# Transposing gathered rows on TensorE with a copy on ScalarE in place of a DMA transpose

## The chip, the cores and the metric

The kernel runs on one core of a Trainium2 chip. The metric is the device time of one execution in microseconds (us). The engines are TensorE (PE), VectorE (DVE), ScalarE (ACT), GpSimd (POOL) and SyncE (SP); SP issues DMAs here, and POOL issues the indirect ones. Each engine works through its own queue in order. An "L" with a number is a line of the kernel.

## The reference

Three layers in a row: attention in chunks of 64 rows, a mixture of 8 experts where each token goes to the expert with the highest gate value, and a feed-forward block (FFN). The change lies in the middle one. x has 2304 tokens of 512 values, an expert's first weight is 512x1024, its second 1024x512.

```python
expert_idx = np.argmax(logits, axis=1)
# the first `capacity` (576) tokens of each expert, in order: disp[e, pos] = x[i]
h = np.maximum(np.einsum('ecd,edf->ecf', disp, w1), 0.0)
y = np.einsum('ecf,efd->ecd', h, w2)
for i in range(N):
    if keep[i]:
        out[i] = gate_w[i] * y[expert_idx[i], pos[i]]
# then FFN: h = x @ w_in; g = h * sigmoid(h); g @ w_out
```

All values are float32 at the inputs. The kernel multiplies in float16 and gets the accuracy from splitting each number into a high and a low half (hi, lo): three products hi·hi, lo·hi and hi·lo per block.

## The kernel before

The attention stage writes the rows of x, split in two f16 halves of 512 values (1024 f16 values and one factor per row), to DRAM (x_d), and a router makes tables of which tokens belong to which expert. The stage of the experts runs from some 143 to 437 us, the FFN from there to the end.

**Tiles.** An expert's tokens are worked on in tiles of 128 rows; a tile is (e, j), expert e and tile j. At most 5 tiles of each expert (NJ) are written out in code; tile (e, 0) always runs, tile (e, j) for j from 1 on stands under a branch on the expert's count (`more`, L930), and a loop (`rest`) takes what lies past them. With this input the experts have 4, 1, 4, 3, 2, 1, 3 and 2 tiles, 20 in all.

A tile goes like this. `gather` (L819, POOL, indirect DMA) fetches 128 rows of x_d into one of four buffers xg. `t_dma` (L830, SP) starts a DMA transpose of the 128x1024 f16 values into mxT, of which there are three, so that the 512 values lie on partitions. `t_f1` (L826, DVE) works out a factor. Layer 1 on PE: 96 matmuls 128x128x128 (L845) in two halves into PSUM tiles mh. After each half ScalarE writes hh (L850), and DVE hl (L851), the high and low half of the rectified result. Layer 2 on PE: 24 matmuls 128x512 (L866) into myp, for f from 0 to 7 two with hh and one with hl; f 0 to 3 use the first half's hh and hl, f 4 to 7 the second's. Then ScalarE and DVE split the result into yr (L874 to L879), and POOL scatters it to y_d (L882).

**What runs beside it.** While an expert is worked on, the weights of the experts behind it are made ready. SP loads a weight as four pieces of 512 KB into buffers st (L134 the first weight, L136 the second). ScalarE squares each piece (L157, result "junk") with a row sum; PE adds these over partitions (L124, `total`); DVE makes a scale of it (L102 to L104); POOL writes the high half in f16 (L172); DVE the low half (L175), after which the buffer st may be loaded again. In the same way DVE rebuilds pieces of the FFN's weights (L794 to L802, buffers fs, loaded by L779; L808 is a square of them on ScalarE). Which piece stands where is laid down by hand: `moe_tile` calls `bg(0)` to `bg(4)` and `nxt(-1)` to `nxt(1)` at fixed places (start of tile; after the first half of layer 1; behind layer 1; at f = 6 of layer 2), and lists of functions (`slots`, `arms`) hang on those. For tile (e, 0), nxt is `nxt0`, for the others the `nxt` of `more`.

**Where the transposes stand.** The DMA transpose of tile (e, j+1) is issued at the start of tile (e, j); that of (e+1, 0) behind layer 1 of (e, 0), ahead of loads of the first weight of expert e+2 in SP's queue. The first, the second and expert 7's second stand apart. Each is also issued for the tile behind an expert's last, which is not run: 28 in this run. Ahead of the first tile 28 matmuls with constants (L927) warm PE up.

**PSUM.** fh_s holds two banks for the FFN, fh0 and fh1; while the experts run, fh0 takes the sums of L124 and fh1 is free.

In the attention stage the kernel already transposes 128x1024 f16 rows on PE, eight blocks (L439), with a copy out of PSUM on DVE or ScalarE (L444).

Of the kernel before, what the change touches and what calls it, by code (L numbers as in the profile page):

```python
# [9 lines left out]
F16 = mybir.dt.float16  # L10
# [12 lines left out]
def attention_moe_ffn_kernel(  # L23
# [15 lines left out]
    nc = tc.nc  # L39
    B, H, S, D = q.shape  # L40
    NT, DM = out.shape
    E = w_gate.shape[1]
    DF1 = w1.shape[2]
    DFF = w_in.shape[1]
    P = 128
# [7 lines left out]
    NJ = 5  # L53
# [716 lines left out]
    ps_s = [mps.tile([P, 4, P], F32, name=f"mh{i}") for i in range(4)]  # L770
    yp_s = [mps.tile([P, DM], F32, name=f"myp{i}") for i in range(2)]

    def f_load(k):
        if k >= 2 * KFF:
            return
        m, c = divmod(k, KFF)
        t = fs_s[k % 3]
        if m == 0:
            nc.sync.dma_start(  # L779
                out=t.rearrange("p (k f) w -> p k (f w)", k=KD),  # L780
                in_=w_in.bitcast(I32).rearrange("(k p) f -> p k f", p=P)[:, :, c * 2 * P:(c + 1) * 2 * P],
            )
        else:
            nc.sync.dma_start(out=t.rearrange("p f w -> p (f w)"), in_=w_out.bitcast(I32)[c * P:(c + 1) * P, :])
# [29 lines left out]
    def slot(e, j):  # L814
        return 2 if j % 2 else e % 2
# [9 lines left out]
        f1 = f1_s[slot(e, j)]  # L825
        nc.vector.tensor_scalar(f1, xg[:, DM:DM + 1], w_fac[e, 0], w_fac[e, 1], ALU.mult, ALU.mult)  # L826

    def t_dma(e, j):
        xg = xg_s[2 * (e % 2) + j % 2]
        nc.sync.dma_start_transpose(out=xT_s[slot(e, j)], in_=xg.bitcast(F16)[:, 0:2 * DM])  # L830

    def moe_tile(e, j, tok_i, c_i, keep, nxt, bg):
        xt, f1 = xT_s[slot(e, j)], f1_s[slot(e, j)]
# [24 lines left out]
        yp = yp_s[1 if j else 0]  # L858
        n = 0
        for f in range(KF1):  # L860
            if f == 3 * KF1 // 4:
                bg(4)
                nxt(1)
            hh, hl = hs[f // 4]
            for lh, part in ((hh, 0), (hh, 1), (hl, 0)):
                nc.tensor.matmul(  # L866
                    out=yp, lhsT=lh[:, f % 4, :], rhs=b[f // 2][:, part, (f % 2) * DM:(f % 2 + 1) * DM],
                    start=(n == 0), stop=(n == 3 * KF1 - 1),
                )
                n += 1  # L870
# [20 lines left out]
        gather(e, j, tabs[:, 0, e, j:j + 1])  # L891

    def t_next(e, j):
        t_dma(e, j)
        t_f1(e, j)

    def rest(e):
# [16 lines left out]
    t_next(0, 0)  # L914
    g_next(0, 1)
    g_next(1, 0)
    t_dma(0, 1)
    w_load(1, 1)
    p10[1]()
    g_next(0, 2)  # L920
# [8 lines left out]
    def more(e, j, arms):  # L929
        with tc.If(n_e[e] > P * j) as cmp:  # L930
            def nxt(k):
                if k < 0 and j + 1 < NJ:
                    t_dma(e, j + 1)
                if k == 0 and j + 1 < NJ:
                    t_f1(e, j + 1)
                if k == 0 and j + 2 < NJ:
                    g_next(e, j + 2)

            moe_tile(
                e, j, *cols(e, j), nxt,  # L940
                lambda k: [f() for f in arms[j][k]],
            )
            if j + 1 < NJ:
                more(e, j + 1, arms)
            else:
                with tc.If(n_e[e] > P * NJ):
                    rest(e)
        left = arms[0] if j == 1 else [f for i in range(j, NJ) for k in range(5) for f in arms[i][k]]
        if left:
            with cmp.Else():  # L950
                for f in left:
                    f()
# [28 lines left out]
    for e in range(E):  # L981
# [23 lines left out]

        def nxt0(k):
            if k < 0:
                if 0 < e < E - 1:
                    t_dma(e, 1)
            elif k == 0:  # L1010
                t_f1(e, 1)
                if last:
                    g_next(e, 2)
                else:
                    t_dma(e + 1, 0)
            elif not last:
                t_f1(e + 1, 0)
            else:
                with tc.If(n_e[e] <= SPLIT0):
                    y0_fac()  # L1020
# [16 lines left out]
            arms[0] = []  # L1037
        more(e, 1, arms)
        if e + 2 == E:
            t_dma(E - 1, 1)  # L1040
            with tc.If(n_e[E - 1] <= SPLIT0):
                y0_load()
    with tc.If(n_e[E - 1] > SPLIT0):
# [211 lines left out]
```

## Time and profile before

| | |
|---|---|
| median of 3 runs | 850.56 us (850.43 to 857.25) |
| profiled execution | 850.38 us, its span in the trace 848.6 us |
| mean granted clock of TensorE | 0.929 |
| busy, us: PE, PE weight loads, DVE, ACT, POOL | 722.5, 440.5, 448.1, 333.2, 359.4 |
| DMA | 103.20 MB, mean 122 GB/s |

The trace holds one execution. A busy time sums an engine's instructions; a wait is the idle time ahead of an instruction, put down to what came last. "x8" behind a row counts instructions that were joined in it. The granted clock is a share of full speed: TensorE has two levels here, 1.2 and 2.4 GHz, shown as 0.50 and 1.00, and means in between.

### The profile page before, as it was taken

The numbers are of one execution on the slowest core, as the hardware profiler recorded it, in microseconds if no ns is written. First come the engines' busy times: TensorE is split into PE (matmuls) and PEld (weight loads), VectorE is DVE, ScalarE is ACT, GpSimd is POOL, SyncE is SP. The second block draws the span as 40 slices with busy tenths as digits, with TensorE's granted clock in tenths as the row PEclk, the third lists the DMA queues.
The fourth block names the chain that finished last, engine by engine and source line by source line (L and its number), as shares of the span: only waits on it lengthen the run. The fifth ranks groups of instructions, "written<-read, shape, count | busy, mean of one in ns | idle before, by whom it ended". The sixth has DMA issues, their size and how long they took to land.

```text
span 848.6 us, 14692 instructions
## 1 busy us (share of the span) xinstructions
PE 722.5 (85%) x5526; PEld 440.5 (52%) x5526; DVE 448.1 (53%) x920; ACT 333.2 (39%) x615; POOL 359.4 (42%) x355
## 2 busy tenths in 40 slices
PE   4798764998489989569798776999999999999995
PEld 3677654765456756447553333444444444565442
DVE  4365886654794758678339999633322223222000
ACT  5586737443443536442134455322232223223010
POOL 3475632524571737665167535544223223212111
PEclk9797955899699999979899999999999999999999
DMA  7988983992986798895635235020001000001000
GB/s 170 230 231 206 191 239 59 306 273 56 303 246 162 177 235 239 241 237 123 135 72 102 73 125 124 1 51 1 1 37 38 1 1 37 14 1 39 13 37 38
DMA packets 133325, 103.20 MB, mean 122 GB/s; under 512 B 85472, under 2 KB 112096, under 8 KB 133216
## 3 DMA queue, kind: packets, MB, share of 16 engines
q1 hardware_dynamic: 126784, 83.41, 40.2%
q0 software_dynamic: 5760, 18.39, 7.3%
q8 instruction: 60, 0.98, 0.5%
q14 instruction: 49, 0.40, 0.2%
q10 hardware_dynamic: 672, 0.02, 0.0%
HBM read 73.45 MB, written 14.71 MB: 104 GB/s over the span
## 4 chain that ended last, share of the span: by engine, by line
PE 30%; DVE 8%; issue 7%; DMA 4%; POOL 2%; ACT 1%; POOLq 0%; ACTq 0%; DVEq 0%
PE ops L1143 14%; PE fh L1115 14%; DMA out_dram<-ob,yrow 3%; DVE g L1126 2%; DVE th L1121 2%; DVE wot L797 1%; DVE wot L802 1%; PE mh L845 1%; DVE wot L794 1%; DVE win L734 1%; DMA y_d<-yr,tabs 1%; PE myp L866 0%; POOL win L751 0%; POOL win L749 0%; POOL win L750 0%
## 5 line engine op out<-in xcount | busy, mean ns | idle before, releaser
L1143 PE MATMUL ops<-wot,gh 128*128 128x512 f16 x576 | 171.3, 379 | 0.0
L1115 PE MATMUL fh<-yT,win 128*128 128x512 f16 (+1 forms) x768 | 156.9, 355 | 7.0 <-DVE g L1126 7.0
L1130 POOL TENSOR_TENSOR gl<-g,gh 128x512 f16<-128x512 f32 (+1 forms) x80 | 91.9, 1151 | 163.8 <-ACT gh L1128 163.8
L1115 PEld LDWEIGHTS <-win 128*128 128x128 f16 x960 | 94.2, 98 | 118.1 <-issue 26.1
L845 PE MATMUL mh<-mxT,wsp 128*128 128x128 f16 x1920 | 125.6, 233 | 17.7 <-PEq L930 9.4
L845 PEld LDWEIGHTS <-wsp 128*128 128x128 f16 x1920 | 123.5, 106 | 24.1 <-issue 19.9
L1143 PE MATMUL ops<-wot,gl 128*128 128x512 f16 x288 | 109.2, 379 | 0.0
L1121 DVE TENSOR_TENSOR th<-fh,rb 128x512 f32<-128x512 f32 (+1 forms) x64 | 39.8, 622 | 130.7 <-PE fh L1115 130.7
L1122 ACT ACTIVATE th<-th,fi 128x512 f32<-128x512 f32 (+1 forms) x80 | 54.3, 679 | 133.8 <-DVE th L1121 132.9
L175 DVE SCALAR_TENSOR_TENSOR wsp<-st,s,wsp 128x1024 f16<-128x1024 f32 x64 | 99.6, 1591 | 6.0 <-POOL wsp L172 6.0
L866 PE MATMUL myp<-wsp,hh 128*128 128x512 f16 x320 | 96.5, 384 | 0.0
L1143 PEld LDWEIGHTS <-gh 128*128 128x128 f16 x576 | 56.4, 98 | 64.1
L172 POOL TENSOR_SCALAR wsp<-st,s 128x1024 f16<-128x1024 f32 x56 | 75.2, 1359 | 20.0 <-DVE inv L104 11.4
L1128 ACT CAST gh<-g 128x512 f16<-128x512 f32 (+1 forms) x80 | 45.9, 574 | 73.2 <-DVE g L1126 54.3
L157 ACT ACTIVATE junk<-st 128x1024 bf16<-128x1024 f32 x64 | 67.4, 1053 | 16.4 <-DMA st<-in_moe_w_dram 15.3
L1126 DVE TENSOR_TENSOR g<-fh,th 128x512 f32<-128x512 f32 (+1 forms) x80 | 50.7, 634 | 38.8 <-ACT th L1122 32.4
L866 PE MATMUL myp<-wsp,hl 128*128 128x512 f16 x160 | 61.6, 385 | 8.2 <-DVE hl L851 8.0
L819 POOL DMA_INDIRECT xg<-x_d,tabs x34 | 45.4, 1336 | 35.2 <-issue 9.5
L882 POOL DMA_INDIRECT y_d<-yr,tabs x20 | 23.5, 1175 | 79.3 <-DVE yr L879 36.8
L851 DVE SCALAR_TENSOR_TENSOR hl<-mh,hh 128x512 f16<-128x512 f32 x40 | 27.5, 687 | 48.3 <-ACT hh L850 48.3
L1115 PE MATMUL fh<-st,win 128*128 128x512 f16 x192 | 43.5, 379 | 10.6 <-DVE g L1126 9.3
L866 PEld LDWEIGHTS <-hh 128*128 128x128 f16 x320 | 30.7, 101 | 29.8 <-ACT hh L850 0.8
(194 smaller groups left out, 849.8 us busy)
## 6 DMA issues: line engine op xcount, KB each, us to landing
st<-in_moe_w_dram SPq DMA_DIRECT2D x64, 512.0 KB, 6.4
fs<-in_moe_w_in_dram SPq DMA_DIRECT2D x16, 512.0 KB, 7.0
fs<-in_moe_w_out_dram SPq DMA_DIRECT2D x16, 512.0 KB, 3.4
vbd<-in_v_dram SPq DMA_DIRECT2D x72, 64.0 KB, 3.4
x_d<-xr SPq DMA_DIRECT2D x9, 512.0 KB, 6.1
ku<-in_k_dram SPq DMA_DIRECT2D x6, 512.0 KB, 5.7
qu<-in_q_dram SPq DMA_DIRECT2D x6, 512.0 KB, 8.3
ku<-in_k_dram SPq DMA_DIRECT2D x2, 384.0 KB, 4.2
```

What stands on the lines that cost most here:

```text
L157: nc.scalar.activation(out=junk, in_=st[c], func=ACTF.Square, accum_out=n2[:, c:c + 1])
L172: hi_eng.tensor_scalar(sp[c][:, 0, :], st[c], s, 1.0, ALU.mult, ALU.mult)
L175: lo_eng.scalar_tensor_tensor(out=sp[c][:, 1, :], in0=st[c], scalar=s, in1=sp[c][:, 0, :], op0=ALU.mult, op1=ALU.subtract)
L845: nc.tensor.matmul(out=ps[:, f4, :], lhsT=a[c][:, part, f0:f0 + P], rhs=xt[:, rc, :], start=(n == 0), stop=(n == 3 * KD - 1),)
L866: nc.tensor.matmul(out=yp, lhsT=lh[:, f % 4, :], rhs=b[f // 2][:, part, (f % 2) * DM:(f % 2 + 1) * DM], start=(n == 0), stop=(n == 3 * KF1 ...
L1115: nc.tensor.matmul(out=hp[:, 0:n], lhsT=wv[:, part, c, :], rhs=yT_t[b](rc, n), start=(i == 0), stop=(i == 3 * KD - 1),)
L1121: nc.vector.tensor_tensor(out=th[:, 0:n], in0=hp[:, 0:n], in1=rb_t[b][:, 0:n], op=ALU.mult)
L1122: nc.scalar.activation(out=th[:, 0:n], in_=th[:, 0:n], func=ACTF.Sigmoid, scale=fi[:, 0:1])
L1126: nc.vector.tensor_tensor(out=g[:, 0:n], in0=hp[:, 0:n], in1=th[:, 0:n], op=ALU.mult)
L1128: nc.scalar.copy(out=gh[:, 0:n], in_=g[:, 0:n])
L1130: nc.gpsimd.tensor_tensor(out=gl[:, 0:n], in0=g[:, 0:n], in1=gh[:, 0:n], op=ALU.subtract)
L1143: nc.tensor.matmul(out=o_t[b][t], lhsT=lh[:, t * P:(t + 1) * P], rhs=wv[:, part, :], start=(f == 0 and i == 0), stop=(f == KFF - 1 and i = ...
```

## The change

`t_dma` is taken out wherever it stood. `x_tr(e, j)` takes its place: eight transposes on PE with the identity as the other operand, into a PSUM tile of one bank (xtp, which is fh1 seen as f16), and one copy of 128x1024 f16 by ScalarE to mxT. The transpose of (e, j+1) now stands behind layer 1 of (e, j), and that of (e+1, 0) at a new place, `nxt(2)`, ahead of f = 4 of layer 2 in (e, 0). That of (0, 0) stands ahead of the warm-up matmuls. Numbers of lines behind the edit move by 2 to 6: layer 1 is L849, layer 2 L872, the transposes are L833 and the copy L834.

```diff
@@ -770,6 +770,8 @@
     ps_s = [mps.tile([P, 4, P], F32, name=f"mh{i}") for i in range(4)]
     yp_s = [mps.tile([P, DM], F32, name=f"myp{i}") for i in range(2)]
 
+    xtp = fh_s[1].bitcast(F16).rearrange("p (c t) -> p c t", c=2 * KD)
+
     def f_load(k):
         if k >= 2 * KFF:
             return
@@ -825,9 +827,11 @@
         f1 = f1_s[slot(e, j)]
         nc.vector.tensor_scalar(f1, xg[:, DM:DM + 1], w_fac[e, 0], w_fac[e, 1], ALU.mult, ALU.mult)
 
-    def t_dma(e, j):
-        xg = xg_s[2 * (e % 2) + j % 2]
-        nc.sync.dma_start_transpose(out=xT_s[slot(e, j)], in_=xg.bitcast(F16)[:, 0:2 * DM])
+    def x_tr(e, j):
+        xh = xg_s[2 * (e % 2) + j % 2].bitcast(F16)
+        for c in range(2 * KD):
+            nc.tensor.transpose(out=xtp[:, c, :], in_=xh[:, c * P:(c + 1) * P], identity=ident16)
+        nc.scalar.copy(out=xT_s[slot(e, j)], in_=xtp)
 
     def moe_tile(e, j, tok_i, c_i, keep, nxt, bg):
         xt, f1 = xT_s[slot(e, j)], f1_s[slot(e, j)]
@@ -858,6 +862,8 @@
         yp = yp_s[1 if j else 0]
         n = 0
         for f in range(KF1):
+            if f == KF1 // 2:
+                nxt(2)
             if f == 3 * KF1 // 4:
                 bg(4)
                 nxt(1)
@@ -891,7 +897,7 @@
         gather(e, j, tabs[:, 0, e, j:j + 1])
 
     def t_next(e, j):
-        t_dma(e, j)
+        x_tr(e, j)
         t_f1(e, j)
 
     def rest(e):
@@ -914,7 +920,6 @@
     t_next(0, 0)
     g_next(0, 1)
     g_next(1, 0)
-    t_dma(0, 1)
     w_load(1, 1)
     p10[1]()
     g_next(0, 2)
@@ -929,9 +934,8 @@
     def more(e, j, arms):
         with tc.If(n_e[e] > P * j) as cmp:
             def nxt(k):
-                if k < 0 and j + 1 < NJ:
-                    t_dma(e, j + 1)
                 if k == 0 and j + 1 < NJ:
+                    x_tr(e, j + 1)
                     t_f1(e, j + 1)
                 if k == 0 and j + 2 < NJ:
                     g_next(e, j + 2)
@@ -1005,14 +1009,15 @@
 
         def nxt0(k):
             if k < 0:
-                if 0 < e < E - 1:
-                    t_dma(e, 1)
-            elif k == 0:
+                return
+            if k == 0:
+                x_tr(e, 1)
                 t_f1(e, 1)
                 if last:
                     g_next(e, 2)
-                else:
-                    t_dma(e + 1, 0)
+            elif k == 2:
+                if not last:
+                    x_tr(e + 1, 0)
             elif not last:
                 t_f1(e + 1, 0)
             else:
@@ -1037,7 +1042,6 @@
             arms[0] = []
         more(e, 1, arms)
         if e + 2 == E:
-            t_dma(E - 1, 1)
             with tc.If(n_e[E - 1] <= SPLIT0):
                 y0_load()
     with tc.If(n_e[E - 1] > SPLIT0):
```

SP's queue, with tile (0, 0), before; st_66 to st_69 are the pieces of expert 2's first weight, xg_2145 is the gather of tile (1, 0), xg_2143 that of (0, 2):

```order
L134 DMA st_66<-in_moe_w_dram 128x1024
L830 DMA_TRANSPOSE mxT_2148<-xg_2145 128x8x128
L134 DMA st_67<-in_moe_w_dram 128x1024
L134 DMA st_68<-in_moe_w_dram 128x1024
L134 DMA st_69<-in_moe_w_dram 128x1024
L930 COMPARE_AND_BRANCH
L830 DMA_TRANSPOSE mxT_2147<-xg_2143 128x8x128
L136 DMA st_70<-in_moe_w_dram 128x2x512
```

The same place after:

```order
L134 DMA st_66<-in_moe_w_dram 128x1024
L134 DMA st_67<-in_moe_w_dram 128x1024
L134 DMA st_68<-in_moe_w_dram 128x1024
L134 DMA st_69<-in_moe_w_dram 128x1024
L935 COMPARE_AND_BRANCH
L136 DMA st_70<-in_moe_w_dram 128x2x512
```

Both transposes are gone from between the loads, and nothing in SP's queue waits for a gather any more.

ScalarE's queue in the same tile, before (hh_2153 and hh_2154 are the two halves of the layer-1 output, st_70 to st_73 the pieces whose squares it takes):

```order
L850 ACTIVATE hh_2153<-mh_2168 128x512
L157 ACTIVATE junk,n_1757<-st_70 128x1024
L157 ACTIVATE junk,n_1757<-st_71 128x1024
L850 ACTIVATE hh_2154<-mh_2169 128x512
L157 ACTIVATE junk,n_1757<-st_72 128x1024
L157 ACTIVATE junk,n_1757<-st_73 128x1024
```

After:

```order
L854 ACTIVATE hh_2153<-mh_2168 128x512
L157 ACTIVATE junk,n_1757<-st_70 128x1024
L157 ACTIVATE junk,n_1757<-st_71 128x1024
L854 ACTIVATE hh_2154<-mh_2169 128x512
L834 COPY mxT_2149<-fh_2136 128x1024
L157 ACTIVATE junk,n_1757<-st_72 128x1024
L157 ACTIVATE junk,n_1757<-st_73 128x1024
L834 COPY mxT_2148<-fh_2136 128x1024
```

The copy for tile (0, 1) has come between hh and the squares, and that for (1, 0) behind them.

TensorE's queue in the middle of layer 2 of the same tile, before (hh_2153 and hl_2155 are the first half, hh_2154 the second):

```order
L866 LDWEIGHTS hl_2155
L866 MATMUL myp_2172<-wsp,hl_2155 128x512
L866 LDWEIGHTS hh_2154
L866 MATMUL myp_2172<-wsp,hh_2154 128x512
L866 LDWEIGHTS hh_2154
```

After, the first of eight pairs of rows that come in there:

```order
L872 LDWEIGHTS hl_2155
L872 MATMUL myp_2172<-wsp,hl_2155 128x512
L833 LDWEIGHTS xg_2145
L833 MATMUL fh_2136<-ident_85,xg_2145 128x128
L833 LDWEIGHTS xg_2145
```

The transposes of the next expert's rows stand between the two halves of layer 2, and what follows them in PE's queue waits for the gather with them.

## Rows read from the trace of the kernel before

**Rows 1.** Windows of the stages: us, busy us (instructions) per engine, clock, DMA share, GB/s.
```profile
150.00:437.00 287.00, 235.38 (x2436) 172.47 (x2437) 183.28 (x357) 117.42 (x236) 150.02 (x118) 0.91 0.78 205
437.00:530.00 93.00, 72.64 (x328) 32.31 (x328) 87.75 (x114) 44.53 (x84) 51.10 (x45) 1.00 0.39 100
530.00:848.00 318.00, 309.26 (x1526) 150.02 (x1526) 83.45 (x152) 78.29 (x130) 88.51 (x96) 0.99 0.07 21
```

**Rows 2.** TensorE's waits, 140 to 435 us: waiting line, awaited one, total us, times, longest.
```profile
PE fh L124 <- ACT junk L157: 12.6, 4, 9.9
PE fh L124 <- DVE win L797: 11.6, 1, 11.6
PE mh L845 <- PEq L930: 9.4, 4, 4.5
PE myp L866 <- DVE hl L851: 8.0, 3, 3.0
PE mh L845 <- DMA st<-in_moe_w_dram: 5.1, 1, 5.1
```

**Rows 3.** Line 830, the transposes: duration ns min/median/max; under it, who waited for it.
```profile
L830 SPq DMA_TRANSPOSE mxT<-xg x28: 1232/1240/3275, 146.6 to 424.2; - x28
...
  PEld L845: 1.8, 1
```

**Rows 4.** SyncE's queue, its waits, 130 to 435 us: total us, times, longest.
```profile
SPq L830 <- DMA xg<-x_d,tabs: 35.8, 12, 8.3
```

**Rows 5.** Timeline of TensorE, attention stage: start us, us from first start to last end.
```profile
41.28 0.61 PE L439 MATMUL xtp<-ident,xr 128*128 128x128 f16 x8
41.83 1.09 PE L348 MATMUL sps<-kbd,qT 128*64 128x128 f32 x16
```

**Rows 6.** Line 444, ScalarE's copies of the attention stage.
```profile
L444 ACT COPY xt<-xtp x4: 992/1012/1013, 126.5 to 130.3; 128x1024 f16<-128x1024 f16 x4
```

**Rows 7.** Timeline of TensorE, starts of tiles (2,1), (2,2) and (2,3) (expert, tile).
```profile
241.00 5.52 PE L845 MATMUL mh<-mxT,wsp 128*128 128x128 f16 x96
...
253.17 5.52 PE L845 MATMUL mh<-mxT,wsp 128*128 128x128 f16 x96
...
263.71 1.50 PE L845 MATMUL mh<-mxT,wsp 128*128 128x128 f16 x24
```

**Rows 8.** Window of the four transposes of line 1087, same shape as line 830's.
```profile
554.00:561.00 7.00, 7.00 (x34) 3.21 (x33) 3.44 (x6) 2.18 (x4) 2.54 (x3) 1.00 0.89 152
```

**Rows 9.** Windows in the gap ahead of expert 2.
```profile
215.00:217.00 2.00, 0.00 (x0) 0.00 (x0) 1.53 (x11) 0.57 (x1) 1.19 (x2) 0.94 1.11 133
217.00:219.00 2.00, 0.00 (x0) 0.00 (x0) 1.85 (x2) 1.15 (x3) 2.00 (x2) 0.50 1.09 391
```

**Rows 10.** Timeline of TensorE, tile (0,1), its sum, start of (0,2).
```profile
163.61 5.52 PE L845 MATMUL mh<-mxT,wsp 128*128 128x128 f16 x96
...
174.98 0.39 PE L124 MATMUL fh<-n,ones 128*128 128x4 f32 x2 [1.74 <-ACT junk L157]
...
177.19 6.50 PE L845 MATMUL mh<-mxT,wsp 128*128 128x128 f16 x96
```

**Rows 11.** Timeline of TensorE, expert 1's layer 2 and the sum ahead of expert 2.
```profile
211.50 0.39 PE L866 MATMUL myp<-wsp,hl 128*128 128x512 f16 x1 [2.94 <-DVE hl L851]
...
225.55 0.56 PE L124 MATMUL fh<-n,ones 128*128 128x4 f32 x2 [11.59 <-DVE win L797]
```

**Rows 12.** Timeline of ScalarE, squares in the same gap.
```profile
219.83 1.06 ACT L157 ACTIVATE junk<-st 128x1024 bf16<-128x1024 f32 x1 [1.68 <-DMA st<-in_moe_w_dram]
...
223.02 1.06 ACT L157 ACTIVATE junk<-st 128x1024 bf16<-128x1024 f32 x1 [2.04 <-DMA st<-in_moe_w_dram]
```

**Rows 13.** Timeline of GpSimd, gather of expert 4's first tile.
```profile
279.58 0.99 POOL L819 DMA_INDIRECT xg<-x_d,tabs  x1 [1.23 <-DMA mxT<-xg]
```

**Rows 14.** Timeline of TensorE, middle of layer 2 of tile (3,0).
```profile
286.43 0.59 PE L866 MATMUL myp<-wsp,hh 128*128 128x512 f16 x2
```

**Rows 15.** Line 819, the gathers.
```profile
DMA to landing us min/median/max: 3.3/6.0/8.7
```

## The prediction

> **What bounds the kernel now.** I read the busy times by stage first [rows 1]. From 530 us to the end TensorE (PE) is busy 309.3 of 318.0 us, and from 437 to 530 VectorE (DVE) is busy 87.8 of 93.0: the last two stages are full on one engine each and touch nothing that the change touches, so they end later or earlier by as much as the expert stage before them does. That stage, 150 to 437 us, is bound by no single engine: PE 235.4 of 287.0, DVE 183.3, the DMA engines 0.78 of the time, at a mean granted clock of 0.91. So I looked for what PE waits for there [rows 2]. The waits are the sums over the weights of the next expert but one (line 124: 12.6 us behind ScalarE's squares, 11.6 put down to a DVE instruction), jumps at the end of an expert (9.4 and 5.1), and the second half of the layer-1 output, hl, from DVE (8.0). None of them is for a transpose.
>
> The third view is the transposes themselves [rows 3]: 28 of them, 1.24 us of issue each on SyncE's queue (SP), and the one wait of TensorE for their data is 1.8 us, its weight loads' at the first tile. So the transposes are hidden today. What they take is SP's time, where the queue stands 35.8 us at them until a gather has landed [rows 4], and DMA time that the weight loads want too.
>
> **What is added.** x_tr puts eight 128x128 f16 transposes on PE and one 128x1024 f16 copy on ScalarE (ACT). The same eight stand in the attention stage: in line 439's row they begin at 41.28, and the next group begins at 41.83 [rows 5], so a block costs 0.55 us, in the other undisturbed places 0.54; I take 0.54. An upper bound is the block's own 0.61 us. It can't be under zero work, but it costs nothing where PE would have waited anyway. The copy is 0.99 to 1.01 us on ACT [rows 6].
>
> The Trainium skill speaks against this: "TensorE: Matmul & The Clock Gate", Part 4: PE-mode transpose, gives about 390 ns for one 128x128 transpose alone and about 275 ns inside a kernel, that is 2.2 us for the eight by estimate, and 42 us over 19 of them. The row shows 0.54 for eight in a row in this kernel; I go by the row.
>
> How many are exposed? By the code 28 blocks run: two in the first tile of each of the experts 0 to 6 (their next tile's, and the next expert's first) and one in every other tile up to each expert's last, which makes 27, and the one at the very start. The tiles run are 4, 1, 4, 3, 2, 1, 3 and 2. A tile with no disturbance takes 10.54 us (253.17 to 263.71), of which 5.52 are layer 1 [rows 7]: its matmuls stand back to back, so there a block is paid in full. Eight are covered: the two of expert 1's and of expert 5's only tile, because the stretch behind ends when the weights' sum is ready, not when PE is; and the two of the first tiles of experts 2 and 6, because the hl waits of 2 to 3 us [rows 2] come behind both and end when DVE is done. If that cover goes (DVE done sooner), they cost 0.54 each. The rest, 27 - 8 = 19, cost 19 x 0.54 = **+10.3**. At the start the mxT wait of 1.8 goes, and a block at a slow clock comes in its place ahead of the warm-up matmuls: **+0.1**.
>
> ACT's copy stands behind the second hh and ahead of the squares in the queue. At 1.0 us against 117.4 busy of 287.0 [rows 1] ACT has room; PE's next use of the copy's result is the next tile. xtp is one bank: the block for the next expert must wait for the copy of the block before. That copy is due some 2 us after layer 1's end (the block, hh's end and 1.0), while the next block comes half of layer 2, 2.5 us [rows 7], later than the first. I count nothing, and one copy at each of seven places (7.0) as the upper bound.
>
> **What is taken away.** Per transpose 256 KB on the DMA engines. The price alone is seen later, where four transposes of the same shape run with nothing beside them: 7.0 us at a share of 0.89 [rows 8], 6.2 us in all, 1.56 each. In the expert stage one falls into 215 to 217 us: the rate is 133 GB/s at a full share, and 391 just after, with loads alone [rows 9]. This is 2.0 us x 1.11 = 2.2 us, ahead of the loads that expert 2 waits for.
>
> By the Trainium skill, "Advanced Engine Details and Errata", X-Bar Transpose (TRN2), such DMAs are as fast as regular ones. The rows disagree, with 133 against 391 GB/s. By the page a transpose would be worth only some 0.75 us of a load's time (an estimate), the gains below would be about halved, and the sum would come to 856.
>
> Gains, place by place:
> - Tiles (0,1) and (0,2): 163.61 to 177.19 is 13.58, 3.04 above a full-speed tile, with a wait of 1.74 for a square behind a late load, and after it layer 1 takes 6.50 in place of 5.52 at a fallen clock [rows 10]. Together 4.0. ACT now has a copy ahead of the same squares, and one block of PE's time is in the sum already; I take **-3.1**.
> - Expert 1's gap: PE stands 11.59 us before 225.55 [rows 11]. The view names a DVE instruction, but the four squares ahead of the sum waited 1.68 and 2.04 us for loads [rows 12]. I take the 2.2 of the transpose: **-2.2** (lower bound 0, upper 3.7).
> - Expert 5's gap is alike, 9.9 in [rows 2]; at the price alone: **-1.6**.
> - Tile (2,1): 241.00 to 253.17 is 12.17, 1.63 above [rows 7], a square's wait among it; most of it, **-1.2**.
> - The two small waits for squares that are left of 12.6 once 9.9 and 1.74 are off, 1.0 in all [rows 2]; half lies in (2,1) already: **-0.5**.
> - The jump after (4,1), 5.1 us with the DMA full, against 4.5 for the longest of the other four [rows 2]: **-0.6**.
> - Expert 6's hl wait and the slow clock after it: half a transpose, **-0.8**, the least sure.
>
> Sum of the gains -10.0, over bounds of 0 to -15. SP's 1.24 us of issue I count at nothing: the loads behind it go out when DVE's last step frees their buffer, and that hides it.
>
> **The sum.** The profiled execution is 850.38 us (span 848.6 and 1.8 around it), against a median of 850.56 of the runs shown. 850.4 + 10.3 + 0.1 - 10.0 = **850.8 us**, no change: what the DMA engines gain is paid back on TensorE.
>
> **Rivals.**
> - Faster, about 840. Every load comes sooner, the two squares' waits in expert 1 go whole (3.7 in place of 2.2), (0,1) and (0,2) give 4.0, (2,1) 1.6, and hl comes earlier in experts 2 and 6 (about 5 us of [rows 2], less four blocks then exposed, 2.2). That gives -15 in place of -10: 846. With fewer waits the clock holds too. PE is busy 235.4 us [rows 1] where 20 tiles of 10.54 would be 210.8; the 24.6 above it bounds what a low clock costs. A third of it back gives 838. Against it: the long gaps remain at 7 to 9 us, and the granted clock is 0.50 within such a gap [rows 9].
> - Slower, about 861: the relief is worth nothing. The loads start when DVE has freed a buffer, and if their latency rather than the DMA engines' share sets their end, no gap shortens and +10.4 stands alone. It decides at the squares: their waits of 1.68 and 2.04 would stay. Against it is the rate in [rows 9].
> - Slower, about 862: PE takes over SP's wait. A transpose in PE's queue blocks every matmul behind it until the gather has landed. SP stood 35.8 us so [rows 4]. For expert 4's first rows the gather is issued at 279.58 [rows 13], and x_tr now stands before the matmul at 286.43 [rows 14]: 6.85 us. A gather takes 6.0 as a median and 8.7 at most [rows 15], so up to 1.85 us are exposed at each of six experts, 11.1 in all. The point is a landing of 6.9 us. Against it: the slow gathers queued behind transposes that are gone, and SP's issue times of those transposes depend on more than the landing.
> - The blocks don't cost 0.54 but 2.2 us, a wait per transpose for the one before: 19 x 2.2 less 10.0 gives about 882. Line 439's row [rows 5] speaks against it.
>
> **Chances.** What a measurement of this kernel can tell from no change is about 1%, 8.5 us. My forecast, with half or all of the gains, 0.64; faster, 0.18; relief worth nothing, 0.10; PE waiting for gathers, 0.06; dear blocks, 0.02. All three slower cases lie above 859, so 0.18 counts as slower. The range is 841 to 861: it reaches nearly to the faster rival's 840 below and, above, to the relief worth nothing, so that some 0.1 is left below and 0.1 above.
>
> **What would show it.** In the profile after, line 833 of the changed kernel should stand as 224 matmuls with 0.54 us from a block to what follows, undisturbed tiles at about 11.1 us (10.54 + 0.54) and 11.6 for first tiles; ACT gets 28 copies of 1.0 us. The gap of expert 1 should be some 2 us shorter, expert 5's 1.6, tile (0,1) near 11.6, and the wait before (0,2)'s sum nearly gone. A PE wait at line 833 for the gather's DMA of more than some 2 us in all would make the second slower rival right; squares' waits for loads unchanged, the first; tiles lengthened by 2 us, the last. Gaps that close by more than 5 us, or a granted clock clearly over 0.91 in the stage, would show the faster one. The end of the expert stage should stand within a few us of 437, and the FFN behind it should be as long as before.

## The result

The changed kernel took 859.18 us as the median of 11 runs (856.64 to 860.89), the kernel before 852.9 us in 11 runs (850.43 to 858.42). The ratio is 1.0061, with a 95% interval of 1.0037 to 1.0084: some 5 us slower, which is within the 1% that was called no change, and clear of zero (the ratio is not that of the two medians, which lie 6.3 us apart). A second set of runs gave 1.0034 (1.0007 to 1.0061). The profiled execution of the changed kernel has a span of 857.3 us, in a run of 859.03; that of the kernel before (848.6 and 850.38) was one of its shortest, 2.5 us under the median of 11.

The stage of the experts in the changed kernel, with the columns of [rows 1]:

```profile
150.00:437.00 287.00, 240.62 (x2655) 182.27 (x2653) 186.73 (x352) 140.07 (x259) 144.00 (x114) 0.92 0.58 180
```

The DMA engines are busy 0.58 of the expert stage in place of 0.78, and ACT 140.1 us in place of 117.4: the parts did what they were meant to. TensorE's waits in it, with the columns of [rows 2]:

```profile
PE fh L124 <- ACT junk L157: 17.2, 3, 8.5
PE mh L849 <- PEq L935: 12.3, 4, 5.3
PE myp L872 <- DVE hl L855: 7.1, 4, 2.7
PE fh L833 <- DMA xg<-x_d,tabs: 6.5, 3, 4.4
PE mh L849 <- issue: 4.6, 2, 3.2
...
PE mh L932 <- issue: 2.1, 1, 2.1
```

The two lines for line 124 (12.6 and 11.6 us before) have become one of 17.2; the jumps took 12.3 in place of 9.4 and the 5.1 behind (4,1), which the view had put down to a DMA. Two waits are new: PE waits 6.5 us for gathers at the transposes of line 833, and 2.1 us before the warm-up matmuls of line 932. Line 833 itself, for [rows 3, 5] (duration of one, its count, first and last):

```profile
L833 PE MATMUL fh<-ident,xg x224: 219/219/314, 149.2 to 437.3; 128*128 128x128 f16 x112
```

One transpose takes 219 ns from start to end, but they overlap: a block stands as 0.61 us in the timeline, and what follows it begins 0.44 us after it. Tile (2,2), for [rows 7]:

```profile
257.44 5.52 PE L849 MATMUL mh<-mxT,wsp 128*128 128x128 f16 x96
262.80 0.61 PE L833 MATMUL fh<-ident,xg 128*128 128x128 f16 x8
263.24 0.59 PE L872 MATMUL myp<-wsp,hh 128*128 128x512 f16 x2
...
268.42 0.78 PE L849 MATMUL mh<-mxT,wsp 128*128 128x128 f16 x11
```

The tile takes 10.98 us in place of 10.54, 0.44 for its block. Eight times the 219 ns of one would be 1.75 us, so a sum with eight times a single one's time goes wrong by a factor of 4. The Trainium skill ("TensorE: Matmul & The Clock Gate", Part 4: PE-mode transpose) gives some 390 ns for one in bf16 alone and some 275 inside a kernel; this case's row has 219 for one in f16.

By stretches, worked out from the starts of the tiles in both profiles (us; "sum" is what the prediction's terms give there):

| stretch | before | after | difference | sum |
|---|---|---|---|---|
| first gather's issue | 142.96 | 145.69 | +2.7 | 0 |
| from there to layer 1 of (0,0) | 7.80 | 9.91 | +2.1 | +0.1 |
| to the start of (1,0) | 49.25 | 46.77 | -2.5 | 2.7 - 3.1 = -0.4 |
| to the start of (2,1) | 41.00 | 43.15 | +2.2 | -2.2 |
| to the FFN's first matmul | 196.0 | 198.9 | +2.9 | 7.6 - 4.7 = +2.9 |
| to the end | 411.6 | 412.9 | +1.3 | 0 |

The first row is not the change's: up to the first gather the kernels are the same, and over the 14 profiles of this study that gather is issued between 143 and 149 us, with the profile of before the earliest of all. The last row varies too, 411.0 to 413.2. Of the other four, three are off by 2 us or more: the start, expert 0 behind it (2.1 us better than the sum) and expert 1 with its gap. The start in the changed kernel, PE's timeline:

```profile
149.23 1.04 PE L833 MATMUL fh<-ident,xg 128*128 128x128 f16 x8 [4.36 <-DMA xg<-x_d,tabs]
150.06 0.53 PE L124 MATMUL fh<-n,ones 128*128 128x4 f32 x2
152.66 3.15 PE L932 MATMUL mh<-ident,ones 128*128 128x128 f16 x28 [2.06 <-issue]
155.60 6.60 PE L849 MATMUL mh<-mxT,wsp 128*128 128x128 f16 x91
```

PE reaches the first block at once and stands there for 4.36 us until the gather has landed. Behind it in its queue are, by the code, a sum (line 124), eight loads of registers and then the warm-ups; ahead of the warm-ups the view has 2.06 us of "issue", a wait for nothing that it shows, and by the code that is where the loads stand. In the kernel before, the warm-ups began 3.1 us after that gather's issue, beside it:

```profile
146.05 3.15 PE L927 MATMUL mh<-ident,ones 128*128 128x128 f16 x28 [3.41 <-DVE tabs L703]
150.76 7.70 PE L845 MATMUL mh<-mxT,wsp 128*128 128x128 f16 x96 [1.57 <-DVE yf L826]
```

The third row is the gap of expert 1 and the tile behind it:

```profile
213.85 0.39 PE L872 MATMUL myp<-wsp,hl 128*128 128x512 f16 x1 [2.03 <-DVE hl L855]
...
224.85 0.56 PE L124 MATMUL fh<-n,ones 128*128 128x4 f32 x2 [8.53 <-ACT junk L157]
225.27 7.81 PE L849 MATMUL mh<-mxT,wsp 128*128 128x128 f16 x96
...
237.32 0.62 PE L833 MATMUL fh<-ident,xg 128*128 128x128 f16 x8 [1.20 <-DMA xg<-x_d,tabs]
...
241.04 0.61 PE L872 MATMUL myp<-wsp,hl 128*128 128x512 f16 x1 [2.67 <-DVE hl L855]
...
245.52 0.74 PE L849 MATMUL mh<-mxT,wsp 128*128 128x128 f16 x5
```

The gap is 8.53 us in place of 11.59 [rows 11], 3.1 less where 2.2 were forecast. But tile (2,0) takes 20.25 us from 225.27, where it took 15.03: PE waits 1.20 us for a gather and 2.67 for hl, and the granted clock is 0.50 from 241 to 246 us (the matmul at 241.04 takes 0.61, the same kind in [rows 11] 0.39). The same tile in the kernel before:

```profile
225.97 7.63 PE L845 MATMUL mh<-mxT,wsp 128*128 128x128 f16 x96
...
238.70 0.39 PE L866 MATMUL myp<-wsp,hl 128*128 128x512 f16 x1 [2.08 <-DVE hl L851]
```

One profile is little to go by here. The second profile of the changed kernel (an execution of 860.89 us) has 9.90, 47.55, 39.73, 203.1 and 412.2 us in the last five rows. Its start is as late, but its gap is 10.70 us, tile (2,0) takes 14.66 with no wait for hl, and the stretch from (1,0) to (2,1) is shorter than before; its loss lies between (2,1) and the FFN. So of the three rows only the start is off by as much in both.

### The profile page after: what moved, and what is told of

It is laid out like the page before. It is cut to its first block, busy times and chain, and to the rows that moved or that the text cites. A ratio compares the mean times of both kernels' runs of the same rounds, so it can differ in the third digit from the quotient of the medians.

```text
span 857.3 us, 15074 instructions
## 1 busy us (share of the span) xinstructions
PE 733.9 (86%) x5750; PEld 452.4 (53%) x5750; DVE 450.1 (53%) x920; ACT 358.2 (42%) x643; POOL 357.4 (42%) x355
## 5 line engine op out<-in xcount | busy, mean ns | idle before, releaser
L849 PE MATMUL mh<-mxT,wsp 128*128 128x128 f16 x1920 | 121.7, 230 | 16.9 <-PEq L935 12.3
L849 PEld LDWEIGHTS <-wsp 128*128 128x128 f16 x1920 | 119.8, 104 | 22.6 <-issue 20.0
L175 DVE SCALAR_TENSOR_TENSOR wsp<-st,s,wsp 128x1024 f16<-128x1024 f32 x64 | 101.7, 1623 | 8.9 <-POOL wsp L172 8.9
L872 PE MATMUL myp<-wsp,hh 128*128 128x512 f16 x320 | 96.5, 383 | 0.0
L172 POOL TENSOR_SCALAR wsp<-st,s 128x1024 f16<-128x1024 f32 x56 | 72.2, 1305 | 21.3 <-issue 9.7
L1130 DVE TENSOR_TENSOR g<-fh,th 128x512 f32<-128x512 f32 (+1 forms) x80 | 50.7, 634 | 38.6 <-ACT th L1126 32.3
L872 PE MATMUL myp<-wsp,hl 128*128 128x512 f16 x160 | 61.6, 385 | 7.1 <-DVE hl L855 7.1
L888 POOL DMA_INDIRECT y_d<-yr,tabs x20 | 26.5, 1327 | 82.0 <-DVE yr L885 32.7
L855 DVE SCALAR_TENSOR_TENSOR hl<-mh,hh 128x512 f16<-128x512 f32 x40 | 27.4, 686 | 43.2 <-ACT hh L854 43.0
L1147 PEld LDWEIGHTS <-gl 128*128 128x128 f16 x288 | 28.2, 98 | 34.0
```

What stands on the lines that cost most here:

```text
L172: hi_eng.tensor_scalar(sp[c][:, 0, :], st[c], s, 1.0, ALU.mult, ALU.mult)
L175: lo_eng.scalar_tensor_tensor(out=sp[c][:, 1, :], in0=st[c], scalar=s, in1=sp[c][:, 0, :], op0=ALU.mult, op1=ALU.subtract)
L849: nc.tensor.matmul(out=ps[:, f4, :], lhsT=a[c][:, part, f0:f0 + P], rhs=xt[:, rc, :], start=(n == 0), stop=(n == 3 * KD - 1),)
L872: nc.tensor.matmul(out=yp, lhsT=lh[:, f % 4, :], rhs=b[f // 2][:, part, (f % 2) * DM:(f % 2 + 1) * DM], start=(n == 0), stop=(n == 3 * KF1 ...
L1130: nc.vector.tensor_tensor(out=g[:, 0:n], in0=hp[:, 0:n], in1=th[:, 0:n], op=ALU.mult)
L1147: nc.tensor.matmul(out=o_t[b][t], lhsT=lh[:, t * P:(t + 1) * P], rhs=wv[:, part, :], start=(f == 0 and i == 0), stop=(f == KFF - 1 and i = ...
```

## The experiments

All ratios are to runs of the kernel before in the same set, with 95% intervals; they are not ratios of the two medians in the row. Rows with the same number under "before" are of one set and compare best with each other.

| kernel | median, us | before, us | ratio |
|---|---|---|---|
| changed | 859.18 | 852.9 | 1.0061 (1.0037 to 1.0084) |
| changed, again | 859.37 | 855.24 | 1.0034 (1.0007 to 1.0061) |
| no transposes at all | 851.62 | 856.79 | 0.9938 (0.9913 to 0.9963) |
| DMA transpose of (0,0) only | 850.02 | 855.24 | 0.9926 (0.9901 to 0.9950) |
| both kinds of transposes | 864.39 | 856.79 | 1.0072 (1.0047 to 1.0098) |
| changed, blocks twice | 860.62 | 856.79 | 1.0059 (1.0028 to 1.0090) |
| changed, first block behind a later gather | 867.12 | 856.79 | 1.0111 (1.0085 to 1.0137) |
| changed, first block among the warm-ups | 857.39 | 856.6 | 0.9992 (0.9966 to 1.0017) |
| before, (0,0) alone on PE | 857.16 | 855.24 | 1.0022 (0.9991 to 1.0053) |
| changed, low half behind hl | 859.6 | 856.6 | 1.0021 (1.0000 to 1.0042) |
| before, low half behind hl | 854.35 | 856.6 | 0.9966 (0.9939 to 0.9993) |
| changed, both moves | 854.89 | 856.6 | 0.9988 (0.9964 to 1.0012) |
| before, both moves | 853.98 | 855.24 | 0.9973 (0.9944 to 1.0001) |

**Relief alone, price alone.** The kernel before without transposes:

```diff
     def t_dma(e, j):
-        xg = xg_s[2 * (e % 2) + j % 2]
-        nc.sync.dma_start_transpose(out=xT_s[slot(e, j)], in_=xg.bitcast(F16)[:, 0:2 * DM])
+        return
...
     g_next(0, 0)
+    for t in xT_s:
+        nc.scalar.copy(out=t, in_=xg_s[0].bitcast(F16)[:, 0:2 * DM].rearrange("p (c t) -> p c t", t=P))
```

> The kernel before without any transposes of gathered rows: line 830 issues nothing, mxT is filled once from the first gathered rows at the start by ScalarE, so the outputs are not the reference's. It shows what the relief of DMA and SP alone is worth, with no price on PE. Theory (the relief is worth 10 us, of which 3 in expert 1's gap come back as waits in tile (2,0)): about 845, 7 below the kernel before's 852.9; gap before expert 2's sum about 8.5 us in place of 11.6, wait for hl in (2,0) some 2 to 3 us longer. First rival (the relief is worth all of 10, nothing is given back): about 843. Second rival (DMA was never the limit): 852.9, gap of 11.6 unchanged.

5 us below the kernel before, half of the 10 in the sum. The stretches of its profile say where: from the first gather to the start of (0,2) it takes 31.5 us (before: 34.2), from (1,0) to (2,1) 44.0 (41.0). The gap got shorter and the tile behind it longer, without one block on PE, as PE's timeline of that kernel shows (line 865 is layer 2, 844 layer 1):

```profile
224.99 0.56 PE L124 MATMUL fh<-n,ones 128*128 128x4 f32 x2 [9.30 <-DVE wsp L175]
225.41 7.05 PE L844 MATMUL mh<-mxT,wsp 128*128 128x128 f16 x96
...
241.25 0.61 PE L865 MATMUL myp<-wsp,hl 128*128 128x512 f16 x1 [5.78 <-DVE hl L850]
...
245.72 4.46 PE L844 MATMUL mh<-mxT,wsp 128*128 128x128 f16 x77
```

Gap 9.30 in place of 11.59, but then 5.78 us of waiting for hl in place of 2.08. So in this kernel expert 1's gain is given back before the next tile begins, as the theory said, and without PE's new work. Over the ten profiles in which VectorE's order is the old one, the gap is 9.9 to 11.6 us in the three with all or nearly all DMA transposes and 7.6 to 10.7 in the seven with none or one, but (1,0) to (2,1) takes 41.0 to 43.2 and 39.7 to 44.0: shorter gaps on average, and no shorter stretch. In size the theory (7) was nearer than its rivals (10 and nothing).

The other half, the changed kernel with the old DMA transposes beside the new:

```diff
+    xD_s = [wot[:, KFF - i, :].bitcast(F16).rearrange("p (c t) -> p c t", t=P) for i in range(3)]
...
+    def t_dma(e, j):
+        xg = xg_s[2 * (e % 2) + j % 2]
+        nc.sync.dma_start_transpose(out=xD_s[slot(e, j)], in_=xg.bitcast(F16)[:, 0:2 * DM])
...
```

> The changed kernel with the DMA transposes put back beside the new ones, at their old places and with results that nobody reads (into memory that is free at that time). It shows the price on PE and ACT with no relief. Theory (price +10.3 for 19 exposed blocks, +2 at the start, relief worth 7): about 865, 12 above the kernel before. Rival (relief worth nothing, the price only some 6): the same 859 as the changed kernel.

1.0072, some 6 us above the kernel before and 1 to 3 above the changed kernel, whose two sets gave 1.0061 and 1.0034. That is nearer to the rival. The relief is worth 5 to 6 us where PE has no blocks, and 1 to 3 with the blocks in. The second number is not clear of zero, and the intervals of the single sets reach from -2 to 6 us, so that the two effects don't simply add is likely, but not shown.

**The blocks' own time.** Every block done twice:

```diff
-        for c in range(2 * KD):
+        for c in [*range(2 * KD)] * 2:
             nc.tensor.transpose(
```

> The changed kernel with every block of eight transposes done twice in a row into the same PSUM tile; the copies stay single. Theory (19 of 28 blocks are paid in full on PE): 8 more transposes take 0.44 us, so 19 x 0.44 = 8.4 us more, about 867.5. Rival (PE has slack in the tiles, and other engines' chains set the time): less than 3 us more, under 862.

The rival was right. The tiles grow about as they should, (2,2) to 11.43 us in PE's timeline of that kernel:

```profile
259.15 5.52 PE L849 MATMUL mh<-mxT,wsp 128*128 128x128 f16 x96
264.51 1.06 PE L833 MATMUL fh<-ident,xg 128*128 128x128 f16 x16
...
270.58 4.63 PE L849 MATMUL mh<-mxT,wsp 128*128 128x128 f16 x80
```

But the ratio is that of the changed kernel. 8.4 us of PE time cost 0 to 2 us; by the intervals some 6 can't be excluded, 8.4 can. In the profile a later wait is shorter: expert 0's four tiles took 50.6 us in place of 46.8, and (1,0) to (2,0) 20.6 in place of 22.9. So the count of 19 exposed blocks was wrong. A block lengthens its tile, and the next wait of PE is shorter for it. This prices PE's time alone, since neither the copies nor the waits for gathers were doubled.

The profiles place some of what the blocks cost all told. From (7,0) to the FFN's first matmul, where two blocks stand (0.9 us), it takes 28.4 to 32.3 us in the eight profiles with blocks in all tiles, and 26.4 to 27.7 in the six others. In seven of the eight PE stands 1.0 to 2.9 us behind the ninth matmul of (7,0)'s layer 1, a wait that the view puts down to "issue" and that none of the six has; the kernel with the blocks twice lacks it too. Before, and then after:

```profile
409.36 8.08 PE L845 MATMUL mh<-mxT,wsp 128*128 128x128 f16 x96 [4.54 <-PEq L930]
...
414.03 0.82 PE L849 MATMUL mh<-mxT,wsp 128*128 128x128 f16 x9 [4.40 <-PEq L935]
416.22 4.00 PE L849 MATMUL mh<-mxT,wsp 128*128 128x128 f16 x36 [1.37 <-issue]
```

What holds PE there is not shown.

**The start.** The first try moved the block behind 14 warm-ups, but left the gather for tile (0,2) ahead of it in the program, which goes into the same buffer; the block then waited for that one, and (0,0) was worked on its rows.

```diff
     g_next(0, 0)
-    t_next(0, 0)
+    t_f1(0, 0)
...
     for i in range(28):
+        if i == 14:
+            x_tr(0, 0)
         nc.tensor.matmul(out=ps_s[2][:, i % 4, :], lhsT=ones16, rhs=ident16)
```

> The changed kernel with one move: the block of transposes for tile (0,0) no longer stands ahead of the register loads and the 28 warm-up matmuls, but after the first 14 of them. Theory (the block at the start holds up PE's queue: PE waits 4.36 us for the gather, and only then loads registers for 2.06 us and warms up for 3.15): layer 1 of (0,0) begins 2.1 us earlier measured from the first gather's issue (7.8 us after it, as in the kernel before, in place of 9.9), and the time falls from 859.2 to about 857. Rival (something else ends last there, DVE's low half of the weights or the gather itself): layer 1 begins 9.9 us after the gather's issue as now, and the time stays at 859.2.

It says nothing on the theory as meant. It shows what a late start costs: layer 1 began 16.4 us after the first gather, 6.5 later than in the changed kernel, and the time was 1.0111, 4 to 7 us above the changed kernel's two sets. The next one puts the gather behind the block:

```diff
     g_next(0, 0)
-    t_next(0, 0)
+    t_f1(0, 0)
...
     p10[1]()
-    g_next(0, 2)
...
     for i in range(28):
+        if i == 14:
+            x_tr(0, 0)
         nc.tensor.matmul(out=ps_s[2][:, i % 4, :], lhsT=ones16, rhs=ident16)
+    g_next(0, 2)
```

> The changed kernel with the first block of transposes behind 14 of the 28 warm-up matmuls, and the gather for tile (0,2) behind it, so that the block reads the rows of tile (0,0). Theory (PE's queue is held up at the start): layer 1 of (0,0) begins 5.5 to 7.8 us after the issue of the first gather, in place of 9.9. The time falls by 2 to 2.5 us at most, since the squares of expert 2's weights, which wait for loads, end some 31 us after the gather and hold up the sum in tile (0,1) then. Rival (it all comes back in tile (0,1)): start as stated, and the time of the changed kernel.

PE's timeline at the start of that kernel (line 933 is the warm-ups):

```profile
149.29 1.65 PE L933 MATMUL mh<-ident,ones 128*128 128x128 f16 x14 [3.41 <-DVE tabs L703]
150.73 1.06 PE L833 MATMUL fh<-ident,xg 128*128 128x128 f16 x8
151.58 1.70 PE L933 MATMUL mh<-ident,ones 128*128 128x128 f16 x14
153.08 6.23 PE L849 MATMUL mh<-mxT,wsp 128*128 128x128 f16 x96
```

No wait at the block any more, layer 1 begins 6.4 us after the first gather, and it is not taken back in (0,1): (0,2) begins 30.9 us after that gather, in the changed kernel 34.0. The ratio fell from 1.0061 and 1.0034 to 0.9992, that is by 4 to 6 us, and with it the loss is gone. These are three sets, and the medians alone (859.2 and 859.4 to 857.4) fell by only 2. Within one set the same move was made on the kernel with the low half behind hl (below): 1.0021 to 0.9988, 3 us, and 4.7 by the medians. So the move is worth some 2 to 6 us, which doesn't tell the theory's 2 to 2.5 from more; the rival, that all of it comes back, doesn't fit. The profile doesn't show the gain at the end: from the first gather to the FFN it is 298.2 us, in the changed kernel's two 298.7 and 300.3, and the profiled executions took 859.01, 859.03 and 860.89.

Is the start worth the same without the rest of the change? The kernel before with that block alone, in that place:

```diff
+    def x_tr(e, j):
+        xh = xg_s[2 * (e % 2) + j % 2].bitcast(F16)
...
-    t_next(0, 0)
+    t_f1(0, 0)
...
+        if i == 14:
+            x_tr(0, 0)
...
+    g_next(0, 2)
```

> The kernel before with one thing of the change, well placed: the transpose of tile (0,0) alone is done on PE, behind 14 of the 28 warm-up matmuls, with the gather for (0,2) behind it; the other 27 transposes stay with the DMA. Theory (what matters of the change is the start: the block's place there cost some 6 us, and the kernel without any transposes gained its 5 us there too): layer 1 of (0,0) begins 5.5 to 6.5 us after the first gather's issue, in place of 7.8 to 10.1, and the time is 2 to 5 us below the kernel before, ratio 0.994 to 0.998. Rival (the start comes back in (0,1), and the relief's gain lay in the rest of the stage): ratio 0.999 to 1.001.

It isn't: 1.0022, no gain, as the rival said. Layer 1 of (0,0) begins 6.9 us after the gather (5.5 to 6.5 were stated), but (0,1) then takes 19.65 us. ScalarE's timeline in that tile (line 858 is hh):

```profile
170.30 1.06 ACT L157 ACTIVATE junk<-st 128x1024 bf16<-128x1024 f32 x1 [3.83 <-DMA st<-in_moe_w_dram]
...
174.26 1.06 ACT L157 ACTIVATE junk<-st 128x1024 bf16<-128x1024 f32 x1 [2.82 <-DMA st<-in_moe_w_dram]
...
175.32 0.58 ACT L858 ACTIVATE hh<-mh 128x512 f16<-128x512 f32 x1
```

ScalarE stands 3.83 and 2.82 us at squares whose loads haven't come, with hh queued behind them. With the DMA transposes still there, expert 0 ends when the loads let it, and (0,2) begins 37.2 us after the gather, later than in the profile of before (34.2). I read it so that an early start is kept only where the relief has brought the loads forward. That fits the next run:

```diff
     def t_dma(e, j):
+        if (e, j) != (0, 0):
+            return
         xg = xg_s[2 * (e % 2) + j % 2]
...
+    for t in xT_s[1:]:
+        nc.scalar.copy(out=t, in_=xg_s[0].bitcast(F16)[:, 0:2 * DM].rearrange("p (c t) -> p c t", t=P))
```

> The kernel before with the DMA transpose of tile (0,0) alone; the other 27 are left out, their mxT tiles hold gathered rows put there once by ScalarE, so the outputs are not the reference's. Theory (the relief's gain lies at the start): ratio to the kernel before 0.998 to 1.001, where the kernel without any transposes had 0.994. Rival (it lies in the rest of the stage, in freed DMA time): 0.993 to 0.996 as without any.

0.9926, as without any transposes; the rival is right and the theory that the relief's gain lies at the start falls. With layer 1 of (0,0) 7.7 us after the gather, (0,2) begins after 31.8. The same stretch over the profiles: 31.5 and 31.8 with relief and no blocks, 30.9 and 32.3 with the first block among the warm-ups, 34.0 to 34.8 in the changed kernel, its second profile and its kin with the first block ahead of them, and 34.2 to 37.2 in the four with the old transposes and at most the first block on PE. So the relief is worth some 4 us in expert 0, and the misplaced block took 3 of them. One profile doesn't fit: with both kinds of transposes, and so with no relief and the misplaced block, it is 33.7.

> The changed kernel once more, on the chip of the other three runs. Both theories: ratio to the kernel before 1.004 to 1.008. Were it under 1.002, the difference between it and the kernel with the first block moved would be one of chips.

1.0034: just under the band, and above 1.002. So by this set too the changed kernel is slower than the one with the moved block (0.9992, of another set), by 0.4%; by the first set it was 0.7%. The two intervals overlap here.

**Where expert 1's gain goes.** In the changed kernel GpSimd runs this chain, on its own time (its timeline):

```profile
224.66 1.86 POOL L888 DMA_INDIRECT y_d<-yr,tabs  x1 [0.17 <-issue]
233.89 0.99 POOL L821 DMA_INDIRECT xg<-x_d,tabs  x1 [7.37 <-DMA fs<-in_moe_w_in_dram]
234.91 4.40 POOL L172 TENSOR_SCALAR wsp<-st,s 128x1024 f16<-128x1024 f32 x4
```

The scatter of (1,0) ends at 226.5, then 7.4 us pass, then the gather for (3,0) and the high halves. In the kernel before the same rows begin at 222.36, 231.55 and 232.56, again 7.33 us apart. From the start of (1,0) to the matmul that waits for hl in (2,0) it is 38.69 us before and 38.67 after, whatever the gap did, and 38.1 to 39.5 in eight of the ten profiles with this order of VectorE. The two others are the kernel with the blocks twice (36.3) and the second profile of the changed kernel, where GpSimd stood 6.11 us in place of 7.37 and PE did not wait for hl. DVE's queue has the low half of the first piece ahead of hl, so hl waits for GpSimd. The move:

```diff
-            slots[1] = [l1s[0], lambda: sq2(0), lambda: sq2(1)]
-            slots[2] = [lambda: sq2(2), lambda: sq2(3), l1s[1], l1s[2], l1s[3]]
+            slots[1] = [lambda: sq2(0), lambda: sq2(1)]
+            slots[2] = [lambda: sq2(2), lambda: sq2(3), *l1s]
```

> The changed kernel, and in the first tile of each expert VectorE's low half of the first weight piece (line 175) stands behind the second hl, no longer ahead of it. Theory (in the gap before expert 2 the change gains 3 us, and tile (2,0) gives them back because hl stands in DVE's queue behind a low half that waits for GpSimd's chain of scatter, 7.3 us of wait, gather and high halves, which runs on its own time): the waits of line 872 for hl (7.1 us in the profile of the changed kernel) fall under 1 us, tile (2,0) becomes some 4 to 5 us shorter as its fallen clock goes too, and the time is 6 to 8 us below the changed kernel's, that is 1 to 3 us below the kernel before's. Rival (the 5 us in (2,0) come from the slow clock and the gather on PE, whatever DVE's order): under 2 us less than the changed kernel.

> The kernel before with the same move on VectorE as in the run above. Theory (hl waits of 8.0 us in experts 1, 2 and 6 come from that order): 4 to 6 us below the kernel before, since 2.9 of the 8.0 lie in expert 1 ahead of a gap that hides them. If the give-back through hl is what cost the change its gain, this kernel and the changed one with the same move differ by 1 us or less, where the two without it differ by 5. Rival (the give-back is something else): they still differ by 4 to 6.

PE's timeline of the changed kernel with the move, from the sum ahead of expert 2 to the start of (2,1):

```profile
230.04 0.56 PE L124 MATMUL fh<-n,ones 128*128 128x4 f32 x2 [12.07 <-ACT junk L157]
230.45 7.11 PE L849 MATMUL mh<-mxT,wsp 128*128 128x128 f16 x96
...
241.31 0.62 PE L833 MATMUL fh<-ident,xg 128*128 128x128 f16 x8 [0.71 <-DMA xg<-x_d,tabs]
...
244.50 1.67 PE L849 MATMUL mh<-mxT,wsp 128*128 128x128 f16 x27
```

The wait for hl is gone from expert 1 and from (2,0), and (1,0) to (2,1) takes 38.3 us in place of 43.2 and, in the kernel before, 36.8 in place of 41.0. So that the order of VectorE's queue makes this wait is shown. In the changed kernel with the move 2.6 us of waits for hl are left in the stage, where under 1 was stated. The time follows by less than the 4 to 5 us of the stretch (1.0061 and 1.0034 to 1.0021; 1 to 0.9966, 3 us), and by less than both theories' 6 to 8 and 4 to 6: from (2,1) to the end of layer 1 of (3,0) it took 2 to 4 us more. And the two kernels with the move still differ by 0.55%, as the rival said. So the wait for hl isn't what set the changed kernel behind the other.

> Both moves in the changed kernel: VectorE's low half behind hl, and the first block of transposes behind 14 warm-ups. Theory: the gains add up, 8 to 10 us below the changed kernel and 3 to 5 below the kernel before. Rival: the start's part comes back in tile (0,1), then as the kernel with the first move alone.

> The kernel before with two moves: the transpose of (0,0) alone on PE behind 14 warm-ups, and VectorE's first low half behind hl in the first tile of each expert. Theory (both gains add): ratio 0.990 to 0.995, the best of all. Rival (later waits for loads take one of them back): 0.996 to 0.998, as with VectorE's move alone.

0.9988 and 0.9973: the moves don't add up to the 0.990 to 0.995 of the theory, nor to 3 us below the kernel before. With the first block well placed, the move of the low half brings 0.04% in the changed kernel by the ratios (0.9992 to 0.9988) and 2.5 us by the medians of that set; which later waits take the rest back wasn't followed up. In the kernel before, the early start again brings nothing (0.9966 and 0.9973), as its rival said. The best of the kernels that compute everything is the kernel before with the low half behind hl, 0.9966, that is faster than either of the two kernels that the study began with.

## Why the forecast held, and which of its terms did not

The class was right (no change of over 1%), and so was the outline, a gain of the DMA engines that PE's queue pays back; the centre was some 5 us too low, and the place of the payment another. That the two sides came out even was in part luck: gains and price were each put at about twice what the runs show, and the two errors cancel; what is left is about the start. By steps:

- **Price of a block**: 0.54 forecast, 0.44 measured, right to 0.1 us. **That 19 blocks are exposed**: wrong. Twice the blocks cost 0 to 2 us instead of 8.4. The argument that matmuls stand back to back in a tile is right for the tile, but the expert's end waits for squares, jumps and loads, and a later PE waits less there. What the blocks cost is seen from the kernels with relief and no blocks (0.9938 and 0.9926) to that with relief, blocks and a good start (0.9992): 0.6%, 5 us over three sets. Between profiles of these kernels some 2 to 3 of them stand in expert 7's two tiles, where two blocks take 0.9. What of the 5 is PE time, copies or waits for gathers wasn't taken apart.
- **The start, +0.1**: the term that failed. It counted the block's time and the wait for mxT that goes, and not what stands behind the block in PE's queue: 2.06 us of "issue" where the register loads stand and 3.15 of warm-ups, which had run beside the gather. Measured +2.1 in both profiles, and 2 to 6 us by the kernels with the block moved.
- **Gains, -10.0**: measured -5 to -6 with no blocks. In expert 0 they were there and larger (4 against 3.1). The gap of expert 1 shrank by 3.1 in the changed kernel's first profile and 2.3 without transposes (2.2 forecast), but by 0.9 in the changed kernel's second. Where it shrank, tile (2,0) took it back: its hl waits for GpSimd's chain, which doesn't begin earlier. The sum treated the end of the gap as the end of the wait.
- **Rivals**: PE taking over SP's wait for gathers happened in small: 6.5 us in three places, 4.36 of it at the start, where it did its harm, 1.20 and 0.95 elsewhere, not 1.85 six times. The prediction's own sign for this rival, more than some 2 us of such waits in all, was met; the rival named the mechanism that did the harm, but not the place, and its 862 was too high. The relief worth nothing fell with the kernel without transposes. The dear blocks fell with the row of 0.44. The faster rival's first part (the gap) happened, the rest didn't; the mean granted clock of the stage went from 0.91 to 0.92.
- **Expected in the profile**: gap 2 us shorter, tiles longer by a block, (0,1) near 11.6 (11.12): seen in the first profile; in the second the gap is 0.9 us shorter and (0,1) takes 13.19. End of the stage near 437: it came at 444.4, of which 2.7 us lie ahead of the stage.

What stays open is what holds GpSimd for 6.1 to 8.2 us between scatter and gather (all fourteen profiles), what holds PE at the start of (7,0), and the split of the blocks' 5 us.

## What to carry to other kernels

Work that is moved to an engine brings its waits into that engine's queue: look first at what stands behind it there, above all at starts, where loads and warm-ups used to run beside the wait. And ask of each shortened gap which chain sets the next wait: one that runs on another engine's time gives nothing back earlier, and in the same way hides added work. The price of added work is measured by doing it twice, what a relief is worth by leaving the old work out, and the two needn't add.

## What the runs showed of the hardware

Eight 128x128 f16 transposes in a row cost PE 0.44 us at full clock, although one takes 219 ns. The stretch before the experts, the same in all kernels here, ended up to 6 us apart from profile to profile, so a few us between two profiles of this kernel say nothing without the stretch they lie in. Nor does one stretch of one profile say much: (1,0) to (2,1) took 43.15 and 39.73 us in two profiles of the same kernel.
